# One batch of a linear-attention and MLP kernel: q prepared first, kv three slots sooner, x transposed by the DMA crossbar, and the next loads issued later

## The chip, the cores and the metric

The kernel runs on one core of one Trainium2 chip. The metric is device time in microseconds (us). Executions of the kernel before lie between 294.1 and 297.5 us, but for one outlier of 1069.77 us, which the median of the first table counts. An execution counts as slow when it is over 1.5% above the fastest of its kernel. The experiments ran in three sessions, in which the kernel before had medians of 296.7, 295.39 and 295.31 us, so ratios compare better across them than medians do. A ratio is the mean time of one kernel's fast runs over the mean of the other's fast runs of the same rounds, so it is not quite the ratio of the medians that are quoted beside it.

## The reference, cut to what matters

```python
def phi(x):
    return np.where(x > 0, x, np.exp(x) - 1.0) + 1.0      # elu(x) + 1
q_p, k_p = phi(q), phi(k)                                   # (8, 8, 576, 64)
kv  = np.einsum('bhsd,bhse->bhde', k_p, v)
z   = np.sum(k_p, axis=2)
num = np.einsum('bhsd,bhde->bhse', q_p, kv)
den = np.einsum('bhsd,bhd->bhs', q_p, z)[..., None] + 1e-06
x   = (num / den)                      # tokens x 512 after a transpose of axes
h   = x @ w_in                         # 512 -> 2048
g   = gelu_tanh(h)
out = g @ w_out                        # 2048 -> 512
```

Each of the 8 batches has 576 tokens: 512 "main" ones, and 64 that are collected over pairs of batches as "rests" ("remainder" in the expectations). A chunk below is a quarter of the 512.

## The kernel before

The two large products run batch by batch. `first_half(j)` computes the hidden values of batch j (16 tiles of 128 hidden features, 4 matmuls each, then a gelu on ScalarE); `second_half(j)` computes the output (16 slots of 4 matmuls). The attention of later batches is put between these matmuls: `at(half, batch, slot, fn)` places `fn` after a slot. The order of instructions on each engine is thus fixed by hand. Batch 2 is prepared inside the second half of batch 1:

```python
def plan_third():
    b = 2
    ...
    def exps():                                  # ScalarE, in this order
        box["k"] = exp_main("k", b)
        box["kr"] = phi_rest("kr", 1)
        box["q"] = exp_main("q", b)
        box["qr"] = phi_rest("qr", 0)
        gelu_table()
    def qtr():                                   # q by the DMA crossbar, sync queue
        qts[b] = pt.tile([P, C, NP, P], BF16, name="qt")
        for c in range(C):
            nc.sync.dma_start_transpose(out=qts[b][:, c], in_=...)
    def kv(i):
        if i == 0:
            box["kv"] = ps_a.tile([P, 2, 512], FP32, name="kv_ps", tag="a")   # 2 buffers
        kv_mm(b, i, box["kv"])
    def nab(c):                                  # n_ps = q' kv, then x = num / den
        ...
    def tx(c):                                   # x by TensorE, copied to xt
        copy = nc.scalar.copy if c < 2 else nc.vector.tensor_copy
        pe_tx(b, c, box["x", c], c < 2, copy)
    ...
```

`qt` and `xt` are q and x transposed; `kv_evac` copies kv_ps to `kvbd`, which n_ps reads. Hidden tiles 12 to 15 of batches 0 and 1 use the same two wide PSUM buffers (tag "a") as kv_ps and n_ps. The sync queue issues, in the order in which the program lists them, q's and x's crossbar transposes and the 1 MB loads of k, q and v of later batches; batch 3's q is transposed after batch 2's x (slot 15 of this half), and is needed in slot 12 of the next. GpSimd issues the loads of the rests (eight of 128 KB in this stretch) as soon as their buffers come free.

```python
plan_prepare(3, (2, 1, 7), (1, 2, 0), None, (1, 2, 1), (2, 1, 15), None, (2, 1, 12))
plan_attention(3, 1, 2, (7, 8, 9, 10), (12, 13, 14, 15))
...
for b in range(4, B):
    at(2, b - 3, 2 if b == 4 else 0, lambda b=b: load_batch(b))
```

Of the kernel before, what the change touches and what calls it, by code (L numbers as in the profile page):

```python
# [9 lines left out]
BF16 = mybir.dt.bfloat16  # L10
# [5 lines left out]
def kernel(  # L16
# [12 lines left out]
    nc = tc.nc  # L29
# [3 lines left out]
    P = 128  # L33
    C = 4
    MAIN = P * C
    REST = S - MAIN
    NP = H // 2
# [11 lines left out]
    pt = ctx.enter_context(tc.tile_pool(name="pt", bufs=2))  # L49
# [13 lines left out]
    def load_main(src, b, name, eng, parts=1):  # L63
        t = pld.tile([P, H, C * D], FP32, name=name, tag="ld")
        hs = H // parts
        for i in range(parts):
            eng.dma_start(  # L67
                out=t[:, i * hs : (i + 1) * hs, :],
                in_=src[b, i * hs : (i + 1) * hs, 0:MAIN, :].rearrange(
                    "h (p c) d -> p h (c d)", c=C  # L70
                ),
            )
        return t
# [28 lines left out]
    def load_batch(b):  # L102
        for n, src in (("k", k), ("q", q), ("v", v)):
            ld[n, b] = load_main(src, b, n + "_x", nc.sync)
# [39 lines left out]
    def gelu_table():  # L144
        nc.scalar.preload_act_table_set("gelu_apprx_tanh_and_others")
# [21 lines left out]
    def exp_into(e, x, hs=slice(0, H)):  # L167
        nc.scalar.activation(  # L168
            e[:, :, hs, :].rearrange("p c h d -> p h c d"), by_chunk(x[:, hs]), AF.Exp
        )  # L170

    def exp_main(name, b):
        e = pe.tile([P, C, H, D], BF16, name=name + "_e")
        exp_into(e, ld[name, b])
        return e
# [13 lines left out]
    def phi_of(x, e, name):  # L189
        xp = pphi.tile([P, x.shape[2] // D, H, D], BF16, name=name)  # L190
        phi_line(xp, x)
        phi_min(xp, e)
        return xp

    def phi_rest(name, m):
        x = ld[name, m]
        e = pe.tile([P, 1, H, D], BF16, name=f"{name}_e{m % 2 if name == 'qr' else ''}")
        exp_into(e, x)
        return lambda: phi.__setitem__((name, m), phi_of(x, e, name + "_p"))
# [10 lines left out]
    def cast_v(b, fn, s=slice(0, H)):  # L210
        fn(  # L211
            out=vps[b % 2][:, s, :, 0:D],
            in_=ld["v", b][:, s].rearrange("p h (c d) -> p h c d", d=D),
        )

    def cast_vr(m, halves=(0, 1)):
        for s in halves:
            r = slice(REST * s, REST * (s + 1))
            nc.vector.tensor_copy(out=vrs[m % 2][s][r, :, 0:D], in_=ld["vr", m][r])

    def kv_mm(b, i, kv_ps, at_i=None):
        i_ps = i if at_i is None else at_i
        kp = phi["k", b].rearrange("p c h d -> p c (h d)")
        kr = phi["kr", b // 2].rearrange("p c h d -> p c (h d)")
        dst = kv_ps[:, i_ps // 2, 2 * E * (i_ps % 2) : 2 * E * (i_ps % 2) + 2 * E]
        for c in range(C):
            nc.tensor.matmul(  # L227
                dst,
                lhsT=kp[:, c, P * i : P * (i + 1)],
                rhs=vps[b % 2][:, 2 * i : 2 * i + 2, c, :],  # L230
                start=(c == 0),
                stop=False,
            )
        nc.tensor.matmul(  # L234
            dst,
            lhsT=kr[:, 0, P * i : P * (i + 1)],
            rhs=vrs[(b // 2) % 2][b % 2][:, 2 * i : 2 * i + 2, :],
            start=False,
            stop=True,
        )  # L240

    def kv_evac(b, kv_ps, bank=None, second=None):
        src = kv_ps[:, :, 0 : 4 * E].rearrange("p a (t u) -> p a t u", u=2 * E)
        dst = kvbds[b % 4].rearrange("p (a t) u -> p a t u", t=2)
        if bank is not None:
            dst = dst[:, bank : bank + 1]
        for hf in range(2):
            r, u = slice(64 * hf, 64 * hf + 64), slice(E * hf, E * hf + E)
            fn = second if hf and second else nc.vector.tensor_copy
            fn(out=dst[r, :, :, u], in_=src[r, :, :, u])  # L250
# [8 lines left out]
    def nab_mm(qt_c, kvbd, n_ps, rows=slice(0, P)):  # L259
        for i in range(NP):  # L260
            nc.tensor.matmul(  # L261
                n_ps[rows, i // 2, 2 * E * (i % 2) : 2 * E * (i % 2) + 2 * E],
                lhsT=qt_c[:, i, rows],
                rhs=kvbd[:, i, :],
                skip_group_check=True,
            )
# [14 lines left out]
    def t_x(x, t_ps):  # L281
        xf = x.rearrange("p a t d -> p (a t d)")
        for i in range(NP):
            nc.tensor.transpose(t_ps[:, i, :], xf[:, P * i : P * (i + 1)], ident)  # L284
# [9 lines left out]
    xts = {}  # L294
# [11 lines left out]
    def first_mm(j, m, h_ps, tok=slice(0, MAIN)):  # L306
        xt = xts[j] if j < B else xt_rest
        for c in range(KM):
            nc.tensor.matmul(  # L309
                h_ps[:, tok],  # L310
                lhsT=w_in_sb[:, c, P * m : P * (m + 1)],
                rhs=xt[:, c, tok],
                start=(c == 0),
                stop=(c == KM - 1),
                skip_group_check=True,
            )

    def first_mm_early(j, m):

        hs[j, m] = ps_ho.tile([P, MAIN], FP32, name="h_ps", tag="ho")  # L320
        first_mm(j, m, hs[j, m], slice(0, MAIN // 2))
# [60 lines left out]
    def pe_tx(b, c, x, one_bank=False, copy=nc.scalar.copy):  # L382

        if c == 0:
            xts[b] = pt.tile([P, NP, MAIN], BF16, name="xt")
        if one_bank:
            t_ps = ps_ho.tile([P, NP, 2, P], BF16, name="t_ps", tag="ho")[:, :, 0]
        else:
            t_ps = ps_a.tile([P, 4, NP, P], BF16, name="t_ps", tag="a")[:, 0]
        t_x(x, t_ps)  # L390
        copy(out=xts[b][:, :, P * c : P * (c + 1)], in_=t_ps)  # L391
# [44 lines left out]
    def at(ph, j, slot, fn):  # L436
        fill.setdefault((ph, j, slot), []).append(fn)
# [157 lines left out]
    def plan_third():  # L595

        b = 2
        box = {}

        def exps():  # L600
            box["k"] = exp_main("k", b)
            box["kr"] = phi_rest("kr", 1)
            box["q"] = exp_main("q", b)
            box["qr"] = phi_rest("qr", 0)
            gelu_table()

        def phis(n):
            phi[n, b] = phi_of(ld[n, b], box[n], n + "_p")

        def cast_vs():  # L610
            cast_v(b, nc.vector.tensor_copy)
            cast_vr(1)

        def qtr():
            qts[b] = pt.tile([P, C, NP, P], BF16, name="qt")
            for c in range(C):
                nc.sync.dma_start_transpose(
                    out=qts[b][:, c],
                    in_=phi["q", b][:, c].rearrange("p h d -> p (h d)"),
                )  # L620

        def kv(i):
            if i == 0:
                box["kv"] = ps_a.tile([P, 2, 512], FP32, name="kv_ps", tag="a")
            kv_mm(b, i, box["kv"])

        def nab(c):
            n_ps = ps_a.tile([P, 2, 512], FP32, name="n_ps", tag="a")
            nab_mm(qts[b][:, c], kvbds[b], n_ps)
            box["x", c] = nab_evac(n_ps)  # L630

        def tx(c):
            copy = nc.scalar.copy if c < 2 else nc.vector.tensor_copy
            pe_tx(b, c, box["x", c], c < 2, copy)

        def early(m):
            first_mm_early(2, m)

        at(1, 1, 10, cast_vs)
        at(1, 1, 11, exps)  # L640
        at(2, 1, 0, lambda: phis("k"))
        at(2, 1, 0, lambda: box["kr"]())
        at(2, 1, 0, lambda: phis("q"))
        at(2, 1, 0, qtr)
        at(1, 2, 3, lambda: box["qr"]())
        for i in range(NP):
            at(2, 1, 8 + i // 2, lambda i=i: kv(i))
        at(2, 1, 9, lambda: kv_evac(b, box["kv"]))
        for fn, c, slot in (
            (nab, 0, 10), (nab, 1, 11), (nab, 2, 12), (nab, 3, 13), (tx, 0, 13),  # L650
            (tx, 1, 14), (tx, 2, 15), (early, 0, 15), (tx, 3, 15), (early, 1, 15),
        ):
            at(2, 1, slot, lambda fn=fn, c=c: fn(c))

    def store(j, t, o_sb):
        if j < B:
# [55 lines left out]
    def second_half(j):  # L712
# [34 lines left out]

    plan_second()
    plan_third()
    plan_prepare(  # L750
        3, (2, 1, 7), (1, 2, 0), None, (1, 2, 1), (2, 1, 15), None, (2, 1, 12)
# [10 lines left out]
    at(1, 2, 8, lambda: box0["qr"]())  # L762
    plan_rest(1, (2, 2, 8), (1, 3, 14))
    for b in range(4, B):
        at(2, b - 3, 2 if b == 4 else 0, lambda b=b: load_batch(b))
    for m in range(2, 4):
        at(2, 2 * m - 3, 3, lambda m=m: load_rests(m, (("kr", k), ("vr", v))))
        at(1, 2 * m - 2, 9, lambda m=m: load_rests(m, (("qr", q),)))
# [34 lines left out]
```

## Time and profile before

| | before |
|---|---|
| median of the runs | 297.1 us (296.88 with the runs made beside the changed kernel) |
| span of the profiled run | 293.4 us |
| TensorE busy | 285.2 us, 97% |
| ScalarE, VectorE, GpSimd busy | 54%, 39%, 12% |
| second half of batch 1 | 66.46 to 83.4 us |
| batch 4's loads issued, last one landed | 76.94, 92.75 us |
| batch 3's first q transposed, first needed | 93.3, 96.25 us |

TensorE has almost no idle time, so an edit pays only by what it takes from TensorE, and costs by every wait that it brings to TensorE. The page's row of the granted TensorE clock, in tenths of full speed for 40 equal slices of the span, is full throughout:

```profile
PEclk9999999999999999999999999999999999999999
```

### The profile page before, as it was taken

The page shows a single profiled execution, that of the slowest core. Times are in us where ns is not written, and L with a number is a line of the kernel's source. Part 1 is how long each engine was busy: PE and PEld are TensorE (multiplying, and loading weights), DVE is VectorE, ACT ScalarE, POOL GpSimd, SP SyncE. Part 2 cuts the span into 40 slices and gives each one's busy share as a digit, 9 for nine tenths or more (in the row PEclk, how much of TensorE's full clock was granted, in tenths as well). Part 3 has the DMA queues.
Part 4 walks back from the last instruction along what each step waited for, and adds up shares of the span by engine and source line. Part 5 has one row for each costly group of instructions (what it writes and reads, how often), then busy time and mean ns, then how long its engine had stood idle before and what let it go on. Part 6 is the DMA issues. An engine that isn't in the chain of part 4 may idle for free.

```text
span 293.4 us, 4220 instructions
## 1 busy us (share of the span) xinstructions
PE 285.2 (97%) x1669; PEld 149.2 (51%) x1698; DVE 114.3 (39%) x189; ACT 158.6 (54%) x221; POOL 36.0 (12%) x56
## 2 busy tenths in 40 slices
PE   8989999999999999999999999999999999999995
PEld 6865456644565544544454445544554444444443
DVE  3676426236486683356125652543231000000002
ACT  4539943679965772567255935682560176017400
POOL 8045458400005200000000000000000000000000
PEclk9999999999999999999999999999999999999999
DMA  7999999994599899539914797304231110021032
GB/s 233 317 373 401 398 365 387 333 365 141 150 344 247 179 283 294 159 61 287 307 64 72 251 306 127 71 3 139 75 60 31 71 71 2 0 96 47 2 72 72
DMA packets 64259, 53.23 MB, mean 181 GB/s; under 512 B 31728, under 2 KB 57584, under 8 KB 64240
## 3 DMA queue, kind: packets, MB, share of 16 engines
q1 hardware_dynamic: 60816, 41.82, 51.1%
q10 hardware_dynamic: 2464, 8.52, 7.8%
q0 software_dynamic: 960, 2.62, 3.1%
q8 instruction: 13, 0.21, 0.3%
q14 instruction: 6, 0.05, 0.0%
HBM read 36.70 MB, written 9.44 MB: 157 GB/s over the span
## 4 chain that ended last, share of the span: by engine, by line
PE 91%; DMA 3%; DVE 3%; issue 1%; SPq 0%; ACT 0%; DVEq 0%
PE h_ps L309 42%; PE o_ps L727 40%; DMA q_x<-in_q_dram 3%; PE n_ps L261 3%; PE kv_ps L227 3%; PE o_ps L696 1%; PE t_ps L284 1%; DVE x L273 1%; DVE kvbd L250 1%; PE kv_ps L234 1%; SPq L67 0%; ACT q_e L168 0%; PE t_ps L255 0%; DVE xt L391 0%; DVE q_p L185 0%
## 5 line engine op out<-in xcount | busy, mean ns | idle before, releaser
L727 PE MATMUL o_ps<-w_out_sb,g 128*128 128x512 bf16 x547 | 123.4, 379 | 0.8 <-issue 0.2
L309 PE MATMUL h_ps<-xt,w_in_sb 128*128 128x512 bf16 (+1 forms) x534 | 118.6, 364 | 0.8
L684 ACT ACTIVATE g<-h_ps 128x512 bf16<-128x512 f32 x144 | 83.7, 602 | 46.6 <-PE h_ps L309 44.9
L727 PEld LDWEIGHTS <-g 128*128 128x128 bf16 x560 | 54.2, 98 | 62.6
L309 PEld LDWEIGHTS <-w_in_sb 128*128 128x128 bf16 x612 | 57.6, 97 | 54.7 <-issue 0.5
L742 ACT COPY o_sb<-o_ps 128x512 f32<-128x512 f32 x18 | 10.5, 585 | 57.8 <-PE o_ps L727 57.8
L740 DVE COPY o_sb<-o_ps 128x512 f32<-128x512 f32 x17 | 11.7, 688 | 64.5 <-PE o_ps L727 57.2
L273 DVE TENSOR_TENSOR x<-n_ps,r 128x512 bf16<-128x512 f32 x36 | 24.9, 691 | 1.2
L250 DVE CAST kvbd<-kv_ps 64x260 bf16<-64x260 f32 (+1 forms) x16 | 6.6, 410 | 39.5 <-PE kv_ps L234 39.4
L168 ACT ACTIVATE k_e<-k_x 128x2048 bf16<-128x2048 f32 (+1 forms) x9 | 15.5, 1721 | 4.7 <-DMA k_x<-in_k_dram 4.6
L168 ACT ACTIVATE q_e<-q_x 128x2048 bf16<-128x2048 f32 (+1 forms) x10 | 15.5, 1557 | 3.5 <-DMA q_x<-in_q_dram 3.5
L271 DVE RECIPROCAL r<-n_ps 128x8 f32<-128x8 f32 x36 | 7.4, 205 | 24.1 <-PE n_ps L261 24.1
L185 DVE TENSOR_TENSOR k_p<-k_p,k_e 128x2048 bf16<-128x2048 bf16 (+1 forms) x9 | 10.5, 1172 | 13.3 <-ACT k_e L168 13.2
L336 PE MATMUL w_ps<-warm 128*128 128x252 bf16 x94 | 13.8, 312 | 1.2 <-DVE warm L127 1.1
L309 PE MATMUL h_ps<-xt_rest,w_in_sb 128*128 128x512 bf16 x62 | 13.9, 379 | 0.1
L261 PEld LDWEIGHTS <-qt 128*128 128x128 bf16 x128 | 9.7, 98 | 7.9 <-issue 1.0
L211 DVE CAST vp<-v_x 128x2048 bf16<-128x2048 f32 (+1 forms) x9 | 9.3, 1042 | 11.0 <-DMA v_x<-in_v_dram 11.0
L261 PE MATMUL n_ps<-kvbd,qt 128*128 128x130 bf16 x128 | 12.7, 221 | 0.6 <-ACT kvbd L250 0.2
L179 DVE TENSOR_SCALAR q_p<-q_x 128x2048 bf16<-128x2048 f32 (+1 forms) x10 | 10.6, 1064 | 6.7 <-DMA q_x<-in_q_dram 6.5
L227 PEld LDWEIGHTS <-k_p 128*128 128x128 bf16 x128 | 9.6, 96 | 6.2 <-DVE vp L211 0.8
L227 PE MATMUL kv_ps<-vp,k_p 128*128 128x130 bf16 x128 | 11.8, 220 | 0.5 <-DVE vp L211 0.5
L336 PEld LDWEIGHTS <-warm 128*128 128x128 bf16 x94 | 10.4, 113 | 3.4 <-DVE warm L127 1.1
(52 smaller groups left out, 140.3 us busy)
## 6 DMA issues: line engine op xcount, KB each, us to landing
out_dram<-o_sb ACTq DMA_DIRECT2D x16, 512.0 KB, 4.9
k_x<-in_k_dram SPq DMA_DIRECT2D x7, 1024.0 KB, 5.9
v_x<-in_v_dram SPq DMA_DIRECT2D x7, 1024.0 KB, 12.1
q_x<-in_q_dram SPq DMA_DIRECT2D x6, 1024.0 KB, 8.6
w_st<-in_moe_w_out_dram SPq DMA_DIRECT2D x4, 1024.0 KB, 11.1
w_st<-in_moe_w_in_dram SPq DMA_DIRECT2D x3, 1024.0 KB, 8.6
q_x<-in_q_dram SPq DMA_DIRECT2D x4, 512.0 KB, 10.0
k_x<-in_k_dram SPq DMA_DIRECT2D x2, 512.0 KB, 4.2
```

The lines of the kernel that those rows point to most:

```text
L168: nc.scalar.activation(e[:, :, hs, :].rearrange("p c h d -> p h c d"), by_chunk(x[:, hs]), AF.Exp)
L179: nc.vector.tensor_scalar(xp[:, :, hs, :].rearrange("p c h d -> p h c d"), by_chunk(x[:, hs]), 1.0, 1.0, op0=ALU.add, op1=ALU.max,)
L185: nc.vector.tensor_tensor(xp[:, :, hs, :], xp[:, :, hs, :], e[:, :, hs, :], op=ALU.min)
L227: nc.tensor.matmul(dst, lhsT=kp[:, c, P * i : P * (i + 1)], rhs=vps[b % 2][:, 2 * i : 2 * i + 2, c, :], start=(c == 0), stop=False,)
L261: nc.tensor.matmul(n_ps[rows, i // 2, 2 * E * (i % 2) : 2 * E * (i % 2) + 2 * E], lhsT=qt_c[:, i, rows], rhs=kvbd[:, i, :], skip_group_che ...
L273: nc.vector.tensor_tensor(x, n_v[:, :, :, 0:D], r[:, :, :, None].to_broadcast([P, 2, 4, D]), op=ALU.mult,)
L309: nc.tensor.matmul(h_ps[:, tok], lhsT=w_in_sb[:, c, P * m : P * (m + 1)], rhs=xt[:, c, tok], start=(c == 0), stop=(c == KM - 1), skip_grou ...
L336: nc.tensor.matmul(w_ps[:, 0:252], lhsT=warm[:, 0:P], rhs=warm)
L684: nc.scalar.activation(gs[j][:, i, :], ps, AF.Gelu_apprx_tanh)
L727: nc.tensor.matmul(o_pss[t], lhsT=g[:, m, P * t : P * (t + 1)], rhs=w_out_sb[:, m, :], start=(m == 0), stop=(m == MM - 1),)
L740: nc.vector.tensor_copy(dst, o_ps)
L742: nc.scalar.copy(dst, o_ps)
```

## The change

The intent is to take batch 2's work off TensorE and to end two short waits. ScalarE and VectorE prepare q first, so its transposes start sooner; kv moves from slots 8 and 9 to 5 and 6, so its copies are done before the first n_ps; x is transposed by the crossbar and no longer by 16 TensorE transposes with four copies; and batch 4's loads are put behind the transposes of x in the sync queue, since these would otherwise stand behind 3 MB of loads.

```diff
         def exps():
+            box["q"] = exp_main("q", b)
             box["k"] = exp_main("k", b)
             box["kr"] = phi_rest("kr", 1)
-            box["q"] = exp_main("q", b)
...
         def tx(c):
-            copy = nc.scalar.copy if c < 2 else nc.vector.tensor_copy
-            pe_tx(b, c, box["x", c], c < 2, copy)
+            if c == 0:
+                xts[b] = pt.tile([P, NP, MAIN], BF16, name="xt")
+            nc.sync.dma_start_transpose(
+                out=xts[b][:, :, P * c : P * (c + 1)],
+                in_=box["x", c].rearrange("p a t d -> p (a t d)"),
+            )
...
+        at(2, 1, 0, lambda: phis("q"))
+        at(2, 1, 0, qtr)
         at(2, 1, 0, lambda: phis("k"))
         at(2, 1, 0, lambda: box["kr"]())
-        at(2, 1, 0, lambda: phis("q"))
-        at(2, 1, 0, qtr)
...
-            at(2, 1, 8 + i // 2, lambda i=i: kv(i))
-        at(2, 1, 9, lambda: kv_evac(b, box["kv"]))
-        for fn, c, slot in (
-            (nab, 0, 10), (nab, 1, 11), (nab, 2, 12), (nab, 3, 13), (tx, 0, 13),
-            (tx, 1, 14), (tx, 2, 15), (early, 0, 15), (tx, 3, 15), (early, 1, 15),
-        ):
-            at(2, 1, slot, lambda fn=fn, c=c: fn(c))
+            at(2, 1, 5 + i // 2, lambda i=i: kv(i))
+        at(2, 1, 6, lambda: kv_evac(b, box["kv"]))
+        for c, slot in enumerate((8, 9, 10, 11)):
+            at(2, 1, slot, lambda c=c: nab(c))
+            at(2, 1, slot, lambda c=c: tx(c))
+        for m in range(4):
+            at(2, 1, 15, lambda m=m: first_mm_early(2, m))
...
-        at(2, b - 3, 2 if b == 4 else 0, lambda b=b: load_batch(b))
+        at(2, b - 3, 12 if b == 4 else 0, lambda b=b: load_batch(b))
```

More of the change, by code (lines that the diff above doesn't have):

```diff
@@ L632, in tx @@
         def tx(c):
-            copy = nc.scalar.copy if c < 2 else nc.vector.tensor_copy
-            pe_tx(b, c, box["x", c], c < 2, copy)
-        def early(m):
-            first_mm_early(2, m)
+            if c == 0:
[4 more added lines that the diff above has]
+            )
         at(1, 1, 10, cast_vs)
         at(1, 1, 11, exps)
+        at(2, 1, 0, lambda: phis("q"))
+        at(2, 1, 0, qtr)
         at(2, 1, 0, lambda: phis("k"))
         at(2, 1, 0, lambda: box["kr"]())
-        at(2, 1, 0, lambda: phis("q"))
-        at(2, 1, 0, qtr)
         at(1, 2, 3, lambda: box["qr"]())
         for i in range(NP):
-            at(2, 1, 8 + i // 2, lambda i=i: kv(i))
-        at(2, 1, 9, lambda: kv_evac(b, box["kv"]))
-        for fn, c, slot in (
-            (nab, 0, 10), (nab, 1, 11), (nab, 2, 12), (nab, 3, 13), (tx, 0, 13),
-            (tx, 1, 14), (tx, 2, 15), (early, 0, 15), (tx, 3, 15), (early, 1, 15),
-        ):
-            at(2, 1, slot, lambda fn=fn, c=c: fn(c))
+            at(2, 1, 5 + i // 2, lambda i=i: kv(i))
[5 more added lines that the diff above has]
+            at(2, 1, 15, lambda m=m: first_mm_early(2, m))
     def store(j, t, o_sb):
```

## The prediction

> **What bounds the kernel now.** I read the page's busy shares and its chain first, then the timeline of all engines from 52 to 90 us (batch 2 is prepared there, inside the second half of batch 1), then the timeline of the sync queue, then the landing times of single transfers.
>
> ```profile
> PE 285.2 (97%) x1669; PEld 149.2 (51%) x1698; DVE 114.3 (39%) x189; ACT 158.6 (54%) x221; POOL 36.0 (12%) x56
> ...
> PE 91%; DMA 3%; DVE 3%; issue 1%; SPq 0%; ACT 0%; DVEq 0%
> ```
>
> TensorE is busy 97% of 293.4 us and is 91% of the chain. So a change counts only by the TensorE instructions it removes and by the TensorE waits it removes or makes. The timeline, in order of time (start, us, engine, line, operation, tiles, count, idle time before):
>
> ```profile
> 65.11 1.91 ACT L168 ACTIVATE k_e<-k_x 128x2048 bf16<-128x2048 f32 x1
> ...
> 71.17 2.06 ACT L684 ACTIVATE g<-h_ps 128x512 bf16<-128x512 f32 x4
> ...
> 77.43 0.24 PEld L261 LDWEIGHTS <-qt 128*128 128x128 bf16 x4 [0.65 <-issue]
> 77.46 0.40 PE L261 MATMUL n_ps<-kvbd,qt 128*128 128x130 bf16 x4 [0.19 <-DVE kvbd L250]
> ...
> 80.99 0.38 PE L284 MATMUL t_ps<-ident,x 128*128 128x128 bf16 x4
> 81.16 0.59 PEld L727 LDWEIGHTS <-g 128*128 128x128 bf16 x4
> 81.21 1.03 PE L727 MATMUL o_ps<-w_out_sb,g 128*128 128x512 bf16 x4
> ...
> 84.72 5.29 PEld L309 LDWEIGHTS <-w_in_sb 128*128 128x128 bf16 x29 [0.25 <-issue]
> ```
>
> The reader should see: four exps end only before 71.17, when ScalarE starts the last four gelus of batch 1; TensorE waits for kvbd before the first n_ps; four transposes hold TensorE from 80.99 to 81.21; and there is a wait of 0.25 us before 84.72, for the last copy of xt. The sync queue and TensorE's later use of what it brings:
>
> ```profile
> 71.67 5.22 SPq L617 DMA_TRANSPOSE qt<-q_p  x4
> 76.94 0.58 SPq L67 DMA_DIRECT2D k_x<-in_k_dram  x1
> 77.63 0.52 SPq L67 DMA_DIRECT2D q_x<-in_q_dram  x1
> 78.25 1.44 SPq L67 DMA_DIRECT2D v_x<-in_v_dram  x1
> 87.19 5.72 SPq L463 DMA_TRANSPOSE qt<-q_p  x4
> ```
>
> ```profile
> 96.25 0.40 PE L261 MATMUL n_ps<-kvbd,qt 128*128 128x130 bf16 x4
> ```
>
> The loads are batch 4's; the transposes at 87.19 are batch 3's q, and TensorE first needs them at 96.25. Issue to landing in us, asked for narrow windows:
>
> ```profile
> v_x<-in_v_dram SPq DMA_DIRECT2D x1, 1024.0 KB, 14.5
> ...
> qt<-q_p SPq DMA_TRANSPOSE x1, 6.1
> ...
> xt_rest<-x SPq DMA_TRANSPOSE x1, 10.3
> ```
>
> Batch 4's v_x lands at 78.25 + 14.5 = 92.75, and batch 3's first qt at 87.19 + 6.1 = 93.3: just after it. With an empty queue the median landing of the xt transposes on the page is 2.4 us. The slack of batch 3's qt is 96.25 - 93.3 = 2.95 us.
>
> **What the Trainium skill says.** "DMA: Bandwidth & Descriptors", section "Queues, rings and completion order": the sync engine owns one ring on each of the 16 DMA engines, and "on each SDMA engine descriptors are consumed in ring order". The trace agrees: qt lands 0.5 us after v_x, and xt_rest, issued behind batch 5's loads, takes 10.3 us in place of 2.4. "VectorE: DVE Perf Modes", section "The three transpose paths", gives 390 ns for a 128x128 transpose on TensorE and 1309 ns by the crossbar. In this trace TensorE transposes overlap: four take (81.21 - 80.99) = 0.22 us of its time, while one crossbar transpose of a whole 128x512 tile takes 1.3 us of the queue (5.22 / 4) and 2.4 to land. "TensorE: Matmul & The Clock Gate", section "Wait — 56ns, not 53.3ns?", gives 55.6 and 215.7 ns from start to start at 128 and 512 columns; 0.22 / 4 = 55 ns agrees, and so do the four o_ps matmuls from 81.21 to the next transposes at 82.07: 0.86 / 4 = 215 ns.
>
> **The change part by part.** One slot of the second half is 4 matmuls x 0.2157 = 0.863 us. Slot 8 ended when kv began (74.22), so the half began at 66.46 and slot 5 ends at 71.63.
>
> *Removed from TensorE:* 4 groups of transposes x 0.22 = 0.88 us. The wait for xt: the early matmuls from 84.04 would be issued by 84.04 + 4 x 0.109 = 84.48, the next start is 84.72: 0.24. The wait for kvbd: the last kv matmul starts at 76.19, four o_ps (one record is missing) follow, so n_ps was due at 76.25 + 0.863 = 77.12 and started at 77.46: 0.34. It goes, since kv now ends two slots (1.73 us) before the first n_ps and its two casts take 0.87. Four half-width first matmul groups in place of two cost 16 x 0.109 x 2 against 16 x 0.109 + 8 x 0.2157: 0.02 more. Gain 1.44 us. Copies of xt (2 x 0.59 on ScalarE, 2 x 0.42 on VectorE) go too, off the path.
>
> *Added, first wait:* kv at slot 5 is due at 71.63. VectorE does the same six feature-map instructions in another order and ends at the same 71.6, with kr_p last, and kr_p is read 0.24 us after the first kv matmul: no wait. But kv_ps takes one of two wide PSUM buffers, which the matmuls of hidden tiles 12 and 13 hold until their gelus. These stand behind the exps, whose sum doesn't change with their order: gelus at 71.17 and 71.67, the second done at 72.26. So kv waits until 72.3: 0.67 us. Net so far 1.44 - 0.67 = 0.77 us gained.
>
> *Crossbar:* n_ps of chunk 3 would start at 71.63 + 0.67 + 4 x 0.295 (kv) + 6 x 0.863 + 3 x 0.235 = 79.36; x follows 1.4 us later (77.46 to 78.83 today). The four xt transposes issue at 77.5, 78.8, 80.1, 81.4 and land by 83.8. The early matmuls on columns 0 to 255 start at 83.05 and run 1.74 us, so chunks 2 and 3 are needed at 84.8: in time by 1 us. q's own transposes start 3.3 us sooner, and are no longer close.
>
> *Loads later:* the sync queue comes to batch 4's loads at 82.7, not 76.94: 5.8 us later. Batch 3's q transposes are still behind them in program order. If all keeps its pace the first lands at 93.3 + 5.8 = 99.1. Part of one 512 KB store now goes before the loads (estimate: 0.7 us less), and GpSimd's loads, eight of 128 KB from 91.5 on, now share engines with the loads' tail (estimate: 0.5 to 1 more). TensorE needs it at 96.25 - 0.77 = 95.5. So it waits some 3.5 us, and the other three chunks, 0.5 to 2.4 us apart, mostly hide behind 1.1 us per chunk.
>
> *Sum:* while TensorE waits for that landing, the end is set by the landing and not by what was gained earlier: 99.0 - 96.25 = 2.8 us longer. All later stages just shift, since TensorE is busy throughout.
>
> **Rivals.** (1) *The loads go faster:* they face a queue without transposes ahead, and the q transposes could land at 96 or earlier. For: the engines moved about 350 GB/s with 1 MB of stores mixed in. And the next two sets of loads took 13.5 and 13.3 us from first issue to last landing, batch 4's 15.8: at 13.4 qt would land at 82.7 + 13.4 + 0.5 = 96.6, a wait of 1 us. Against: those sets met one store of 512 KB, these meet two, and 4 MB at that rate are 12 us in any order. With no second wait at all it is 297.1 - 0.8 = 296.3. (2) *The PSUM wait does not come*, because the gelus end sooner or the buffer is another: 0.67 us more gain before the landing, so 295.6 together with rival 1, and nothing if the landing binds. (3) *The crossbar transposes are slowed* by the stores from 82 us on, landing after 84.8: up to 1 us, mostly swallowed by the later wait. (4) *TensorE cools:* the same TensorE page, in "Part 1: The HAM clock gate", halves the clock after an idle window of about 3.4 us. No stretch of this trace after the start shows a lower clock (its row has 9 throughout), but a wait of 3.5 us comes near; one window at half clock would add about 1.7 us and give 301.5.
>
> **Range and chances.** I weight the late landing at 70%, rival 1 at 25%. The centre of the landing case is 297.1 + 2.8 = 299.9, of the other 296.3; the weighted value is 298.9. The three runs of before are 295.5 and 297.1 besides an outlier, so 1 us of noise either way: 295.2 to 302.0. Two per cent is 5.9 us; the largest gain is below 1.5 us, and a loss above 5.9 needs cooling and a long wait together: faster 0.01, within 0.93, slower 0.06.
>
> **What would show it.** Right: the t_ps group of batch 2 gone from TensorE; kv_ps starting near 72.3 after a wait for the gelu; no wait before the first n_ps of batch 2; loads issued near 82.7; the first qt of batch 3 landing 0.5 us after v_x near 99, and TensorE idle for about 3 us before the n_ps of batch 3, in the first half of batch 2. Wrong: no idle time there, or qt landing before v_x; then the end is earlier by about 0.8 us. If kv starts at 71.7, the PSUM step is wrong. A lower clock after the wait would be rival 4.

## The result, and the profile after

The changed kernel takes 307.35 us in the median (306.53 to 308.16, 4 runs) against 296.88 us: ratio 1.0368, 95% interval 1.0319 to 1.0418. It is slower by over 3%, outside the range of the prediction. The results are correct.

| | before | after |
|---|---|---|
| median | 296.88 us | 307.35 us |
| span of the profiled run | 293.4 us | 306.4 us |
| second half of batch 1 starts | 66.46 us | 67.77 us |
| batch 4's loads issued | 76.94 us | 84.00 us |
| batch 4's last load landed | 92.75 us | 104.1 us |
| batch 3's first q landed | 93.3 us | 106.0 us |
| mean granted clock | 1.0 | 0.983 |

The second half of batch 1 starts 1.3 us later in the profiled run after. That comes from waits for weights near the start, ahead of everything that the change touches, so I take it off when I compare times of day in the two traces. From that start to the end the spans differ by 306.4 - 67.77 - (293.4 - 66.46) = 11.7 us.

On the page, the busy shares, the clock and the chain answer to those of before:

```profile
PE 287.4 (94%) x1661; PEld 150.0 (49%) x1690; DVE 112.9 (37%) x187; ACT 157.5 (51%) x219; POOL 36.2 (12%) x56
...
PEclk9999999999999669999999999999999999999999
...
PE 74%; DMA 15%; ACT 4%; SPq 4%; issue 1%; DVE 1%; POOL 0%; ACTq 0%
```

TensorE has 8 matmul records less, as 16 transposes went and 8 half-width matmuls came, and yet it is busy for longer: two slices of 7.7 us each ran at about 0.6 of the clock. In the chain DMA has gone from 3% to 15%. TensorE's waits from 66 to 120 us, longest first (total, times, longest):

```profile
PE n_ps L261 <- DMA qt<-q_p: 7.8, 1, 7.8
PE h_ps L309 <- DMA xt<-x: 1.2, 1, 1.2
PE kv_ps L227 <- ACT g L685: 0.5, 1, 0.5
```

All three were named in the prediction: the first as the late landing of batch 3's q, the second as rival 3, the third as the PSUM buffer. The first is more than twice as long as predicted. TensorE's timeline around it:

```profile
96.64 1.67 PE L309 MATMUL h_ps<-xt,w_in_sb 128*128 128x512 bf16 x6
106.12 0.62 PE L261 MATMUL n_ps<-kvbd,qt 128*128 128x130 bf16 x4 [7.80 <-DMA qt<-q_p]
106.53 1.91 PE L309 MATMUL h_ps<-xt,w_in_sb 128*128 128x512 bf16 x4
```

After 106.12, four matmuls take 1.91 us, where four at full clock take 1.02. The clock record of the trace is 0.5 from 101.64 to 111.88 us. The sync queue, in order of time:

```profile
78.82 5.13 SPq L635 DMA_TRANSPOSE xt<-x  x4
...
84.00 0.72 SPq L67 DMA_DIRECT2D k_x<-in_k_dram  x1
...
85.71 2.03 SPq L67 DMA_DIRECT2D v_x<-in_v_dram  x1
...
87.84 15.43 SPq L463 DMA_TRANSPOSE qt<-q_p  x4
```

and the landing times (issue to landing, us) of that v_x and of the first of those four transposes:

```profile
v_x<-in_v_dram SPq DMA_DIRECT2D x1, 1024.0 KB, 18.4
...
qt<-q_p SPq DMA_TRANSPOSE x1, 18.2
```

The loads come behind x's transposes, at 84.00, which is 82.7 in the time of the trace before. Batch 3's q comes behind the loads, and its four issues alone hold the queue for 15.4 us, where they took 5.7 before. v_x lands at 85.71 + 18.4 = 104.1 and the first qt at 87.84 + 18.2 = 106.0. TensorE resumes 0.1 us after that.

### The profile page after: what moved, and what is told of

Its sections match the earlier page's. It is cut to its first block, busy times and chain, and to the rows that moved or that the text cites. A ratio compares the mean times of both kernels' runs of the same rounds, so it can differ in the third digit from the quotient of the medians.

```text
span 306.4 us, 4211 instructions
## 1 busy us (share of the span) xinstructions
PE 287.4 (94%) x1661; PEld 150.0 (49%) x1690; DVE 112.9 (37%) x187; ACT 157.5 (51%) x219; POOL 36.2 (12%) x56
## 4 chain that ended last, share of the span: by engine, by line
PE 74%; DMA 15%; ACT 4%; SPq 4%; issue 1%; DVE 1%; POOL 0%; ACTq 0%
PE o_ps L728 35%; PE h_ps L309 32%; DMA qt<-q_p 6%; DMA w_st<-in_moe_w_out_dram 4%; DMA k_x<-in_k_dram 3%; PE n_ps L261 3%; SPq L67 2%; PE kv_ps L227 2%; DMA xt<-x 2%; ACT k_e L168 1%; PE o_ps L697 1%; ACT L145 1%; SPq L76 1%; SPq L90 1%; ACT q_e L168 1%
## 5 line engine op out<-in xcount | busy, mean ns | idle before, releaser
L309 PE MATMUL h_ps<-xt,w_in_sb 128*128 128x512 bf16 (+1 forms) x542 | 121.0, 366 | 2.0 <-DMA xt<-x 1.2
L309 PEld LDWEIGHTS <-w_in_sb 128*128 128x128 bf16 x620 | 59.0, 99 | 56.7 <-issue 1.9
L741 DVE COPY o_sb<-o_ps 128x512 f32<-128x512 f32 x17 | 11.7, 689 | 65.5 <-PE o_ps L728 58.2
L261 PE MATMUL n_ps<-kvbd,qt 128*128 128x130 bf16 x128 | 13.4, 229 | 8.2 <-DMA qt<-q_p 7.8
L336 PEld LDWEIGHTS <-warm 128*128 128x128 bf16 x94 | 10.2, 111 | 3.2 <-DVE warm L127 1.1
## 6 DMA issues: line engine op xcount, KB each, us to landing
q_x<-in_q_dram SPq DMA_DIRECT2D x4, 512.0 KB, 10.5
```

Of the source, the lines that this page charges most:

```text
L261: nc.tensor.matmul(n_ps[rows, i // 2, 2 * E * (i % 2) : 2 * E * (i % 2) + 2 * E], lhsT=qt_c[:, i, rows], rhs=kvbd[:, i, :], skip_group_che ...
L309: nc.tensor.matmul(h_ps[:, tok], lhsT=w_in_sb[:, c, P * m : P * (m + 1)], rhs=xt[:, c, tok], start=(c == 0), stop=(c == KM - 1), skip_grou ...
L336: nc.tensor.matmul(w_ps[:, 0:252], lhsT=warm[:, 0:P], rhs=warm)
L741: nc.vector.tensor_copy(dst, o_ps)
```

## The experiments

My theory after the result: the loss is the wait for batch 3's q behind the delayed loads, made longer by GpSimd's loads, and dearer by the half clock that follows a long idle time. The main rivals: crossbar transposes or the traffic as such cost the time wherever they stand; the later slot of the loads itself is at fault; the half clock has another cause. "Waits" below are those of TensorE in the stretch of interest.

### Experiment 1: the loads behind batch 3's q

```diff
-        at(2, b - 3, 12 if b == 4 else 0, lambda b=b: load_batch(b))
+        at(2, b - 3, 15 if b == 4 else 0, lambda b=b: load_batch(b))
```

> One edit to the changed kernel: batch 4's loads go from slot 12 to slot 15, where they stand behind batch 3's q transposes in the sync queue. Queue theory (mine): nearly all of the loss is the wait of TensorE for batch 3's first qt, idle 98.2 to 106.1 us in the changed kernel's profile, and the half clock of 10.2 us after it; both end, the first qt lands by 91 us, the clock stays 1.0, and what is left is the 0.7 us wait for kv_ps and at most 1.4 us for the last xt: 296 to 299 us, ratio 1.00 to 1.01. Rival (the crossbar transposes of x or the DMA bandwidth as such cost the time): the ratio stays at 1.02 or more. A new wait could come at batch 4's exps, which need k_x near 98 us.

Measured: 302.84 us, ratio 1.0237 (1.0179 to 1.0294). The waits, as the trace gives them:

```profile
PE n_ps L261 <- DMA qtr<-qr_p: 5.5, 1, 5.5
PE kv_ps L227 <- ACT g L685: 0.5, 1, 0.5
PE h_ps L309 <- DMA xt<-x: 0.3, 1, 0.3
```

The wait for batch 3's qt is gone, so it was made by the loads ahead of it, by their place in the queue or by their bytes. But the time did not come back as I expected: the next thing in the queue, the transpose of a rest's q (qtr), now stands behind the loads. It was issued at 96.07, landed at 107.5 and TensorE idled 5.5 us for it, with 6.8 us of half clock. I had foreseen a wait of ScalarE for k_x (it came, 1.8 us, and cost TensorE nothing that shows) and not this one. The loads are 3 MB wherever they stand, and whatever follows them in the queue pays.

### Experiment 2: the rests' loads by the sync queue

```diff
-        at(2, 2 * m - 3, 3, lambda m=m: load_rests(m, (("kr", k), ("vr", v))))
-        at(1, 2 * m - 2, 9, lambda m=m: load_rests(m, (("qr", q),)))
+        at(2, 2 * m - 3, 3, lambda m=m: load_rests(
+            m, (("kr", k), ("vr", v)), nc.gpsimd if m == 2 else nc.sync))
+        at(1, 2 * m - 2, 9, lambda m=m: load_rests(m, (("qr", q),), nc.sync))
```

(`load_rests` takes the engine as an argument.)

> One edit to the changed kernel: the eight 128 KB loads that GpSimd issues between 91.3 and 96.0 us (q's remainder of pair 2, all of pair 3) are issued by the sync queue in program order, so they no longer share the DMA engines with the tail of batch 4's loads. In the changed kernel v_x landed 20.1 us after the first load's issue minus 1.7, at 104.1; before it took 15.8 from the first issue. Theory (GpSimd's loads are what my estimate of 0.5 to 1 us undersized): v_x lands near 100 us, the first qt of batch 3 half a us later, TensorE idles 2 to 4 us in place of 8, and with so short a wait the clock stays at 1.0 or is low for less than 10 us: 300 to 302 us. Rival (stores and the loads themselves make it slow): v_x lands at 103 or later and the time stays near 307.

(The figure in its second sentence is muddled: from the first load's issue it took 20.1 us.)

Measured: 298.13 us, ratio 1.0054 (1.0012 to 1.0097): nearly all of the loss is gone, more than I expected. Landing times of batch 4's v_x and batch 3's first qt in this run, issued at 84.46 and 86.60:

```profile
v_x<-in_v_dram SPq DMA_DIRECT2D x1, 1024.0 KB, 13.6
...
qt<-q_p SPq DMA_TRANSPOSE x1, 12.0
```

From the first load's issue (82.75) to v_x's landing (98.06) it took 15.3 us; in the changed kernel it took 104.1 - 84.0 = 20.1. TensorE waits 1.6 us for qt in place of 7.8, and the clock stays full. What GpSimd's loads did is to be seen in the bytes and the time that each queue had in six microseconds while the loads were under way (packets, MB, share of the 16 engines). The changed kernel, 95 to 101 us, where q0 is GpSimd's queue and q1 the sync queue:

```profile
q0 software_dynamic: 304, 0.87, 63.0%
q1 hardware_dynamic: 930, 0.90, 58.1%
```

and experiment 2, 91 to 97 us:

```profile
q1 hardware_dynamic: 2390, 2.05, 121.8%
```

(The shares are of the time that packets took, and can go over 100%.) With GpSimd's loads the sync queue moved 0.90 MB in the time in which it otherwise moves 2.05. Over the whole stretch from the first load's issue to v_x's landing, all queues moved 5.55 MB in the changed kernel, 1.02 of them GpSimd's, and 4.53 MB in experiment 2, at 276 and 296 GB/s. At the latter rate 1.02 MB take 3.4 us: most of the 4.8 us is the mere bytes, and the rest the lower rate. Other runs agree: the stretch took 20.4 and 21.6 us in experiments 5 and 12, which keep GpSimd's loads, and 16.1 in experiment 6, which does not. In experiment 2 the sync queue issues these loads only from 99.70 us on, after qt has landed; so it shows what they cost in the way, and not whether 1 MB from another queue would cost less. In the kernel before the eight were issued at nearly the same times, from 91.54 us on, but batch 4's last load landed 1.2 us after that (92.75). The change moved the loads into their way.

### Experiment 3: x by TensorE again, all else of the change kept

The edit takes back the `tx` hunk and the early matmuls of the diff (TensorE transposes at slots 13 to 15, two early groups); q first, kv at slots 5 and 6, n_ps at 8 to 11 and the loads' slot 12 stay.

> The changed kernel with x transposed by TensorE as before (slots 13 to 15, two early matmul groups), everything else of the change kept, the loads' slot 12 too. Queue theory: the sync queue has nothing to wait for between q's transposes and the loads, so the loads issue near 75.5 us although their slot is 12; what made them late was waiting behind x's transposes, not the slot. First qt of batch 3 lands by 94, no wait for it, clock 1.0; against before it saves the 0.34 us wait for kvbd and the 0.24 for the last xt, and pays 0.7 for kv_ps: 296 to 298 us, ratio 0.995 to 1.005. Rival (the slot itself delays the loads): loads issued after 82 us and the loss of 10 us stays.

Measured: 296.44 us, ratio 1.000 (0.9949 to 1.0052). The sync queue:

```profile
72.73 2.57 SPq L617 DMA_TRANSPOSE qt<-q_p  x2
75.35 0.58 SPq L67 DMA_DIRECT2D k_x<-in_k_dram  x1
```

The loads follow q's transposes at once, at 75.35, although their slot is 12: a slot orders instructions within an engine, and this queue had nothing left to wait for. So the slot did not delay the loads; standing behind x's transposes, each of which waits for VectorE's x, did. The only wait left is the 0.5 us for the PSUM buffer.

### Experiment 4: the loads back at slot 2, x by the crossbar

```diff
-        at(2, b - 3, 12 if b == 4 else 0, lambda b=b: load_batch(b))
+        at(2, b - 3, 2 if b == 4 else 0, lambda b=b: load_batch(b))
```

> The changed kernel with batch 4's loads back at slot 2, so ahead of x's crossbar transposes in the sync queue. Queue theory: loads issue near 75.5 us, v_x lands near 91, all four xt of batch 2 land right behind it at 91 to 94, and TensorE, which needs the first two at 84.4, idles about 8 us there, then runs at half clock for some us as after the wait of 8 us in the changed kernel; batch 3's q comes in time later: 304 to 309 us. Rival (crossbar transposes overtake loads): they land 2.4 to 4 us after issue and the time is 297 or less, which would make the later slot a mistake.

Measured: 302.83 us, ratio 1.0221 (1.0174 to 1.0269), a little less bad than expected.

```profile
PE h_ps L309 <- DMA xt<-x: 6.0, 1, 6.0
```

The first xt took 9.8 us from issue to landing (77.69 to 87.48, behind v_x at 85.80), and the half clock lasted 3.4 us. Without the later loads, x is what waits. Even so this version loses less than the changed kernel (1.0221 against 1.0368, the intervals are apart): in the change as it stands, moving the loads made things worse. None of the places tried in this queue, slots 2, 12 and 15 and slot 4 of the next half (experiment 7), was free.

### Experiments 5 and 12: dummy matmuls in the wait

```diff
+    at(1, 2, 12, lambda: keep_warm(24))        # experiment 12: 37
     plan_attention(3, 1, 2, (7, 8, 9, 10), (12, 13, 14, 15))
```

> The changed kernel with 48 dummy matmuls of 252 columns (some 5.2 us of TensorE, 0.108 us each) put ahead of batch 3's first n_ps, that is into the wait of 8 us. The landing of qt is not touched, so TensorE still goes on near 106 us; only its idle time falls to about 3 us. Theory (the half clock from 101.6 to 111.9 us follows from the idle time and costs 5.8 us x 1/2 = 2.9 us of the loss): clock 1.0 throughout, 303.5 to 305 us, ratio to before about 1.026. Rival (the clock falls for another reason, or its cost is hidden): time stays at 307 or gets worse.

> Experiment 5 with 74 dummy matmuls (8.0 us) in place of 48, which should fill nearly the whole wait for batch 3's qt. Experiment 5 left 2.7 us idle and the clock was still halved for 3.4 us after it. Theory (idle time alone halves the clock): no half clock after the wait; against the changed kernel's 307.35 us 2.9 us are won back, to 304 to 305; the landing of qt stays where it was. Rival: the half clock comes all the same, or the dummies run past the landing and the time doesn't change from experiment 5's 305.96.

Measured: experiment 5 took 305.96 us, ratio 1.0374 (1.0323 to 1.0425); experiment 12 took 304.39 us, ratio 1.0292 (1.0247 to 1.0336). The clock rows of the two, experiment 5 and then experiment 12:

```profile
PEclk9999999999999989999999999999999999999999
```

```profile
PEclk9999999999999999999999999999999999999999
```

and their waits for batch 3's q:

```profile
PE n_ps L261 <- DMA qt<-q_p: 2.7, 1, 2.7
```

```profile
PE n_ps L261 <- DMA qt<-q_p: 0.5, 1, 0.5
```

Experiment 5 left 2.7 us idle (101.8 to 104.4), and 0.9 us after TensorE had resumed the clock was halved for 3.4 us. Its median is 1.4 us below the changed kernel's, its ratio is not below, so its time is inconclusive, and its rival is not excluded by the time. Experiment 12 left 0.5 us idle; no half clock followed and the landing (104.65, in a run whose kv_ps started 2.2 us sooner) came 0.8 us later by that measure. It is 3.0 us faster than the changed kernel by the medians of two sessions, 0.0076 x 296 = 2.2 us by the ratios, whose intervals overlap a little. The traces settle it. From batch 3's first n_ps to the end of the span the changed kernel takes 306.4 - 106.12 = 200.3 us, experiment 5 303.5 - 104.42 = 199.1, experiment 12 302.1 - 104.70 = 197.4, and the kernel before 293.4 - 96.25 = 197.2. In the changed kernel's trace TensorE works from 106.12 to 111.88 at half clock, which is 5.76 / 2 = 2.9 us of lost time. So the half clock follows from the idle time, and is 2.9 us of the loss by the traces.

### Experiment 6: experiment 2 with a store held back

```diff
-                if j == B or t % 2 == 1:
+                if j == 1 and t == 1:
+                    held = o_sb
+                elif j == B or t % 2 == 1:
+                    if j == 1:
+                        store(j, 1, held)
                     store(j, t, o_sb)
```

> Experiment 2 (remainder loads by the sync queue) with one more edit: the first 512 KB store of batch 1 is held until the second, so that it is issued near 84 us and not at 82.2, when the last two crossbar transposes of x are under way. In experiment 2 the fourth xt took 4.7 us to land (81.47 to 86.19) where the three before took 2.4, and TensorE idled 1.2 us for it. Theory (the store in flight is what holds it): the fourth xt lands 2.4 to 3 us after issue, the 1.2 us wait goes; the wait for batch 3's qt stays near 1.6 us or grows a little, as the store now mixes with the loads: 296 to 298.5 us. Rival (the loads queued behind slow it): it still lands after 85.5 us.

Measured: 300.83 us, ratio 1.0191 (1.0145 to 1.0237). The step that it was made for came out as expected. Issue to landing of the fourth xt in the changed kernel (with the store beside it, whose own line is in the same answer) and in experiment 6:

```profile
out_dram<-o_sb ACTq DMA_DIRECT2D x1, 512.0 KB, 3.8
xt<-x SPq DMA_TRANSPOSE x1, 4.7
```

```profile
xt<-x SPq DMA_TRANSPOSE x1, 2.4
```

and the 1.2 us wait for xt is gone. The sum was worse all the same: both stores now ran among the loads, the first qt landed at 100.0, TensorE idled 3.7 us for it, and the clock was halved for 6.8 us. My expectation of "a little" growth of that wait was too small.

### Experiment 7: four mends at once

Loads after batch 3's q and the rest's q (slot 4 of the next half), rests by the sync queue, all kv at slot 6, and chunk 3 of x by TensorE at slot 13:

```diff
+            if c == 3:
+                pe_tx(b, c, box["x", c], False, nc.vector.tensor_copy)
+                return
...
-            at(2, 1, 5 + i // 2, lambda i=i: kv(i))
+            at(2, 1, 6, lambda i=i: kv(i))
...
-        at(2, b - 3, 12 if b == 4 else 0, lambda b=b: load_batch(b))
+        at(*((1, 2, 4) if b == 4 else (2, b - 3, 0)), lambda b=b: load_batch(b))
```

> The change with four mends: batch 4's loads after the q transposes of batch 3 and of the remainder (first half of batch 2, slot 4), the remainder loads by the sync queue, all kv of batch 2 at slot 6 so that the gelus have freed its PSUM buffer, and chunk 3 of x transposed by TensorE two slots later. If the waits seen so far are all there is, TensorE keeps 3 groups of transposes less (0.66 us) and loses the waits for kvbd and xt (0.58): about 1.2 us faster than before, 295 to 296.5 us, ratio 0.994 to 1.0. Rival (later loads again find something behind them, as in experiment 1): TensorE idles at batch 4's exps or before n_ps of the remainder or of batch 4, and the ratio is above 1.003.

Measured: 298.13 us (297.84 without the one slow execution, 301.73), ratio of fast runs 1.0086 (1.0036 to 1.0137). The rival came true, one batch later:

```profile
PE n_ps L261 <- DMA qt<-q_p: 2.3, 1, 2.3
```

This wait is at 123.9 us, for batch 4's q. All waits in batch 2's preparation are gone, but batch 5's loads are issued at 109.73, 6.8 us later than in the kernel before (102.89), and batch 4's q stands behind them.

### Experiment 8: experiment 3 with all kv at slot 6

```diff
-            at(2, 1, 5 + i // 2, lambda i=i: kv(i))
+            at(2, 1, 6, lambda i=i: kv(i))
```

> Experiment 3 (x by TensorE, all else of the change) with all four kv groups at slot 6. Experiment 3 still idled 0.51 us for the PSUM buffer, held by hidden tiles 12 and 13 until the second gelu after the exps. Theory: at slot 6 (0.86 us later) the buffer is free, so no idle time before kv_ps, none for kvbd and none for the last xt: 0.6 us faster than before, ratio 0.995 to 1.0. Rival (it is kr_p or another operand that kv waited for): the idle time before kv_ps stays.

Measured: 294.97 us against 295.39, ratio 0.9996 (0.9958 to 1.0035). The trace has no wait of TensorE from 66 to 130 us. This alone does not name what kv_ps had waited for, as anything ready 0.7 us later would do. The changed kernel's timeline does: k_p and kr_p were done at 72.07 and 72.93 us, and kv_ps began at 73.64, 0.65 us after the second gelu had started (72.99; a gelu takes 0.60). That is the PSUM buffer. A gain of 0.6 us would be a ratio of 0.998; these runs do not resolve it. It is the same as before within noise, as experiments 3 and 11 are.

### Experiments 9 and 10: batch 4's loads from ScalarE's queue

```diff
-            ld[n, b] = load_main(src, b, n + "_x", nc.sync)
+            ld[n, b] = load_main(src, b, n + "_x", nc.scalar if b == 4 else nc.sync)
```

Experiment 10 adds kv at slot 6 and chunk 3 by TensorE, as in experiment 7.

> One edit to the changed kernel: batch 4's three loads are issued from ScalarE's queue in place of the sync queue, at the same slot 12. Nothing is moved less; only batch 3's q transposes no longer stand behind the loads in one queue. Queue-order theory: they share the engines and land 2.4 to 6 us after issue, before 95 us; no idle time at batch 3's n_ps, clock 1.0; x's last two transposes are shared with loads and stores too, so TensorE may wait 1 to 3 us for xt: 297 to 300 us, ratio 1.00 to 1.012. Rival (it is the bytes in flight, not the order): qt lands after 98 us all the same and the ratio stays at 1.02 or more.

> Experiment 9 with all kv groups at slot 6 and chunk 3 of x transposed by TensorE, as in experiment 7. If queue order was the cause and nothing else waits, TensorE keeps three groups of transposes less (0.66 us) and loses the waits for kvbd and xt (0.58 us): up to 1.2 us faster than before, 294.5 to 296 us, ratio 0.995 to 1.000. Rival (shared engines slow x's third crossbar transpose or batch 3's fourth): a wait of 1 us or more and a ratio of 1.00 to 1.01.

Measured: 301.45 us, ratio 1.0194 (1.0153 to 1.0235), and 302.65 us, ratio 1.0232 (1.0192 to 1.0273). Both missed my expectation. The timeline of ScalarE in experiment 9 shows one reason:

```profile
74.23 1.91 ACT L168 ACTIVATE k_e<-k_x 128x2048 bf16<-128x2048 f32 x1
74.29 0.40 ACTq L67 DMA_DIRECT2D k_x<-in_k_dram  x1
...
78.48 1.28 ACT L145 ACT_TABLE_LOAD   x1
```

In the program the loads follow the table load that runs at 78.48; they were issued at 74.29, when three instructions that stand before them (q_e, qr_e and the table load) had not begun. The queue ran ahead of the engine. So the loads ran under x's transposes and not after them. The wait for batch 3's qt was gone, and TensorE waited 4.1 us for xt instead (4.8 in experiment 10), with 6.8 us of half clock in both. The first xt took 7.4 us to land, from another queue than the loads, against 9.8 behind them in experiment 4 and 2.4 without them. So another queue does not shield a transpose: by this comparison the bytes in flight cost more of the delay (5.0 us) than the place in the queue (the other 2.4). As the timing of the loads is not the same as in the changed kernel, these two runs do not separate order from bytes for batch 3's q itself.

### Experiment 11: the first two parts alone

The kernel before with q's exp and feature map first, and kv at slots 5 and 6 with its copies:

```diff
+            box["q"] = exp_main("q", b)
             box["k"] = exp_main("k", b)
             box["kr"] = phi_rest("kr", 1)
-            box["q"] = exp_main("q", b)
...
-            at(2, 1, 8 + i // 2, lambda i=i: kv(i))
-        at(2, 1, 9, lambda: kv_evac(b, box["kv"]))
+            at(2, 1, 5 + i // 2, lambda i=i: kv(i))
+        at(2, 1, 6, lambda: kv_evac(b, box["kv"]))
```

> The kernel before with the first two parts of the change alone: q's exp and feature map first, and kv with its copy at slots 5 and 6. Theory: the 0.34 us wait for kvbd goes and a 0.5 to 0.7 us wait for the PSUM buffer of kv_ps comes; the sync queue is as before. 0.2 to 0.4 us slower at most, ratio 0.998 to 1.003, the same within noise. Rival (the order of q and k itself costs): an idle time for kr_p or k_p before kv_ps, and a ratio above 1.005.

Measured: 295.22 us, ratio 0.9989 (0.9953 to 1.0025): the same. Its one wait is the 0.5 us for kv_ps that the gelus release. The loss is in the other two parts.

## Why the prediction was wrong

The mechanism and its place were predicted; the range was missed by the size of two terms. A loss above two per cent had been given a chance of 0.06.

**Part removed, and the first wait.** Right. The transposes of batch 2 are gone, the wait for kvbd is gone, kv_ps starts 0.69 us late (73.64 against 67.77 + 6 x 0.863 = 72.95), and the trace names the gelu; 0.67 had been predicted. The timeline shows that the buffer is the cause, and the wait is gone in experiment 8.

**Crossbar.** The fourth xt was to land by 83.8, a microsecond before its use. It landed at 87.4, 86.1 in the time of before, and TensorE waited 1.2 us. The rival that said so named the stores, and experiment 6 shows it. As the prediction said of this rival, the later wait swallows it.

**Loads later.** "The sync queue comes to batch 4's loads at 82.7": 84.00 - 1.31 = 82.69. "If all keeps its pace the first lands at 93.3 + 5.8 = 99.1", less 0.7 for the store: in experiment 2, without GpSimd's loads in the way, it landed at 98.6 (its stretch began within 0.1 us of that of before). This step was right to half a microsecond.

**The step that failed first** is the term "GpSimd's loads, eight of 128 KB from 91.5 on, now share engines with the loads' tail (estimate: 0.5 to 1 more)". With them the first qt landed at 106.0 - 1.3 = 104.7, against 98.6 without: it is 6.1 us, not 0.5 to 1. Of these 4.8 are a longer way of the loads (20.1 against 15.3 us), and 1.3 a larger gap between v_x's landing and qt's (1.9 against 0.6). The estimate does not follow from the prediction's own numbers: all eight loads were to be issued between 91.5 us and the landing near 99, and 1 MB at its 350 GB/s is 3 us. I had counted only a part of them, as sharing the tail. In fact all 1.02 MB passed before v_x had landed, which is 3.4 of the 4.8 us; for six microseconds they took about half of the engines' time, and the sync queue moved 0.90 MB where it moves 2.05 without them.

**The second term** is cooling. I had it as rival 4, for a wait of 3.5 us, at 1.7 us (an estimate: half of the window that the prediction cites from "TensorE: Matmul & The Clock Gate", "Part 1: The HAM clock gate") and outside the centre. With the wait of 7.8 us it came in all four executions (mean clock 0.983 to 0.987), and it cost 2.9 us by the trace, 2.2 to 3.0 by experiment 12.

**The sum with the measured terms.** The prediction's own form was: the end shifts by the landing less 96.25. With the measured landing this is 104.7 - 96.25 = 8.5 us, and with 2.9 for the half clock 11.4. The spans from the start of the stretch differ by 11.7, the medians by 10.5. Experiment 2 takes away 6.2 us of the wait and all of the half clock, 9.1 in all; its median is 9.2 below the changed kernel's, measured in another session.

**Rivals.** Rival 1, that the loads might go faster, failed: they went slower. Rival 2, no PSUM wait, failed. What stays open is how the delay of batch 3's q divides between its place in the queue and the mere bytes in flight: experiments 1, 3 and 2 show that it needs the loads in front of it and, for four fifths of the wait, GpSimd's loads, and experiment 9 shows that transposes in another queue are slowed too. And no version tried beats the kernel before: what the change frees on TensorE is at most 1.4 us of 296, hardly more than the half width of these intervals (1.1 to 1.5 us).

## What to carry to other kernels

When a transfer is moved later, list everything that is issued behind it and beside it in its new place, on all queues, until the bytes have landed; a microsecond freed on the busy engine is soon lost to the first of these that is late. All the bytes of another engine's queue that are issued before your transfer lands should be counted as if they stood ahead of it: here they were 1.02 MB and 4.8 us, of which a count of bytes gives 3.4. And a predicted idle time of several microseconds on TensorE should be given its half-clock cost in the centre of the estimate, since the two come together.

## What the Trainium skill lacked or had wrong

- "TensorE: Matmul & The Clock Gate", "Part 1: The HAM clock gate", puts the fall to half clock after an idle window of about 3.4 us. Here one idle time of 2.7 us was enough (experiment 5), while idle times of 1.6 (experiment 2) and 2.3 us (experiment 7) were not followed by it in the profiled executions. Two others of experiment 7, not profiled, had mean clocks of 0.994 and 0.989, so these runs give no sharp limit. The spells at half clock lasted 3.4, 6.8 or 10.2 us, that is 1, 2 or 3 of the page's windows, after idle times of 2.7 to 8 us.
- "DMA: Bandwidth & Descriptors", section "Rules for kernel authors", says that a transpose next to ordinary DMAs needs nothing. That is so for its result (all runs were correct), but it gives no time: a crossbar transpose of 128x512 took 2.4 us to land alone, 4.7 beside one store of 512 KB, 7.4 beside 3 MB of loads from another queue, 9.8 behind such loads in its own queue, and 18.2 (19.5 in experiment 12) behind them with GpSimd's loads beside them.
- The same page says that queues interleave on the 16 engines; it has no figure for what one queue loses by that. In 6 us GpSimd's 128 KB loads moved 0.87 MB, and the sync queue 0.90 in place of the 2.05 MB that it moved without them.
- No page says outright that a DMA placed in ScalarE's program after several activations may be issued before they run: in experiment 9 the first load was issued at 74.29 us, ahead of three instructions that stand before it, the last of which started at 78.48.
